# Two more groups of w2's sums made during attention, K's token sums merged into one tile, z on the scalar engine, first results turned at a later step

## The chip, the cores and the metric

One core of one Trainium2 chip runs the whole kernel. The metric is the device time of one launch in microseconds. TensorE (PE in the profile) does the matrix products, VectorE (DVE) and ScalarE (ACT) the elementwise work, GpSimd (POOL) small operations and one of the DMA queues, and SyncE (SP) issues most other DMAs. Each engine works through its own instructions strictly in the order in which the kernel wrote them, so an instruction that waits holds up everything behind it on its engine.

## The reference, cut to what matters

```python
# x: 2048 tokens x 512; H = 32 heads of 16; F = 1792; all float32
h   = layernorm(x) * (1 + ca) + sa            # sa, ca, ga, sb, cb, gb = silu(c) @ w_mod
q, k, v = h @ wqkv                            # per head
pq, pk = phi(q), phi(k)                       # phi(t) = (t + 1 if t > 0 else exp(t)) + 1e-6
kv  = sum over tokens of pk * v               # 16 x 16 per head
z   = sum over tokens of pk                   # 16 per head
o   = (pq @ kv) / (pq . z + 1e-6)
x   = x + ga * (o @ wo)
h   = layernorm(x) * (1 + cb) + sb
x   = x + gb * (mish(h @ w1 + b1) @ w2)
```

## The kernel before, in words

**Precision.** Products run in float32r, which keeps fewer bits than float32. Each operand is therefore split into an upper and a lower part: `split` (L144 to L157) rounds a tile to float32r (the upper part, names ending in `h`, mostly on ACT) and subtracts (the lower part, names ending in `l`, on DVE). A product takes three matmuls: upper by upper, upper by lower, lower by upper.

**Stages.** The 2048 tokens are four blocks `b` of 512, each of four tiles `t` of 128. (1) Normalisation, K and the sums `gacc` over tokens, block by block. (2) z and Q of blocks 0 and 1 (`q_sevens`), the small matrices `kv` and `m`. (3) Attention for each block: `attend` makes the denominators (`den`, then `rden`), sends them through DRAM (`rden_d`) and reads them back spread over partitions (`rd`), scales and splits q (`qs`); `o_unit` multiplies. (4) The MLP. (5) The last down products and the output.

**Seven products for eight.** Q of blocks 0 and 1, and both layers of the MLP, multiply two by two blocks with seven products in place of eight. The sums and differences of blocks that this needs have short names: s1 to s4 for the left operand, t1 to t4 for the right. For the down layer the right operand is w2, in seven groups `g` of two 128-row slices. From its raw rows `w2_blocks` and `blocks_job` make the plain blocks (stored to DRAM as `w2d`), and `sums_job` (L1425) makes the differences: two loads `w2q` for groups from `EARLY` = 3 on (the first three reuse the rows loaded for the plain blocks), four subtractions of 128x256 on DVE (L1446), two roundings on ACT (L1292), two subtractions of 128x512 for the lower parts (L1298, tiles `t_3l` and so on by group number), and four stores to DRAM (`w2t`, L1456). `right_job` (L1461) loads them back as `wt_m` when a product needs them. For groups from `EARLY` on, the right operand of the product `m4` comes straight from SBUF in the first pass.

**z before.** `k_post` makes phi(k) of one tile into `ku[b, t]`. For blocks 1 and 2 an accumulating DMA on the POOL queue adds `ku[b, t]` to `ku[0, t]` (L382); for block 3, DVE does (L380). So four tiles remain. `z_unit` sums each over its 128 tokens with a matmul against 32 columns of ones, the four results lying in four quarters of the partitions; ACT and DVE split the result into `zsum`; `z_side` adds the quarters with two more matmuls (`zbc`, L786), and then DVE makes four diagonals, scales the four parts of `hmask`, and makes the four `zs` tiles.

**Order.** Up to the MLP the order is written out in the code. Steps are Python generators; `spawn` hands one over and `tick` advances all of them by one step after each unit of PE's work. In the MLP a planner (`add_job`, `best_job`, `drive`) writes the order: each job has an earliest time and a due time, worked out from a model with the constants in `T`, and of the jobs that can start on an engine the one with the earliest due time is written next. The model's time is not the chip's; only the order reaches the chip. Two streams feed PE: `main_stream` (up products, PSUM tiles `p_a`, `p_s`) and `fill_stream` (down products, tiles `pa`, `pb`, `pc`, `pd`), for the token blocks 0 and 1 (`L` = 0) and then 2 and 3 (`L` = 2).

**Results.** `result_job` (L1640) gathers a finished down product on DVE (L1645, tile `q`), turns it by a 32x32 transpose (L1656, tile `turned`) and adds it to the tokens in DRAM with accumulating DMAs on POOL (L1666, `x1d<-turned`).

**SBUF.** Nearly all tiles of 128x512 come from one pool of 93 slots (`SLOTS`). A new tile takes a slot that an older one gave up, and its first instruction waits until the last use of the older tile, which can be a DMA that still reads it, has ended.

**Steps that the change and the prediction touch.** The ticks inside `q_sevens`: `result` adds the kept copy on DVE (`cq`, L490) and spawns `phi`, whose exp and relu run on ACT (L370, L371); `copy` (tile `qu`, L497) keeps an unfinished sum on ACT before PE adds the next product to the same PSUM tile. `beside_q` loads the residual rows `r` (L165) on SP, and `mod_side` loads `wm` (L176).

The functions that the diff touches, and what calls them, with the line numbers of the profile:

## Time and profile before

| | us |
|---|---|
| median of 3 runs (lowest, highest) | 481.19 (481.16, 481.33) |
| profiled execution, its own time | 481.08 |
| its span | 479.4 |
| PE busy in the span | 469.5 |
| DVE busy in the span | 421.7 |
| ACT busy in the span | 322.0 |
| POOL busy in the span | 161.0 |

The span runs from the first to the last instruction of the profiled execution; 1.7 us of its own time lies outside. An engine's busy time is the union of its instructions. Matmuls overlap, so a record of one 128x512 float32r matmul shows 0.39 us while one starts every 0.23 us. The granted TensorE clock is 0.998.

### The profile page before, as it was taken

The page shows a single profiled execution, that of the slowest core. Times are in us where ns is not written, and L with a number is a line of the kernel's source. Part 1 is how long each engine was busy: PE and PEld are TensorE (multiplying, and loading weights), DVE is VectorE, ACT ScalarE, POOL GpSimd, SP SyncE. Part 2 cuts the span into 40 slices and gives each one's busy share as a digit, 9 for nine tenths or more (in the row PEclk, how much of TensorE's full clock was granted, in tenths as well). Part 3 has the DMA queues.
Part 4 walks back from the last instruction along what each step waited for, and adds up shares of the span by engine and source line. Part 5 has one row for each costly group of instructions (what it writes and reads, how often), then busy time and mean ns, then how long its engine had stood idle before and what let it go on. Part 6 is the DMA issues. An engine that isn't in the chain of part 4 may idle for free.

```text
span 479.4 us, 7265 instructions
## 1 busy us (share of the span) xinstructions
PE 469.5 (98%) x2300; PEld 385.4 (80%) x2300; DVE 421.7 (88%) x825; ACT 322.0 (67%) x586; POOL 161.0 (34%) x238
## 2 busy tenths in 40 slices
PE   8999999999999999999999999998999999999996
PEld 6788887877887888888888888786888888888886
DVE  6989999899789898999979999998986686989995
ACT  6777686865653988769979999476557566547150
POOL 4583320000022413233542132632331236638430
PEclk9999999999999999999999999999999999999999
DMA  8997689143895446545999373996341469999987
GB/s 310 401 355 210 178 163 270 30 148 94 284 210 150 143 152 226 170 135 179 256 349 308 116 219 121 252 290 217 109 155 51 125 176 244 221 319 242 370 156 162
DMA packets 78881, 99.07 MB, mean 207 GB/s; under 512 B 31538, under 2 KB 51770, under 8 KB 78811
## 3 DMA queue, kind: packets, MB, share of 16 engines
q1 hardware_dynamic: 51528, 54.42, 37.3%
q0 software_dynamic: 24000, 43.15, 34.7%
q10 hardware_dynamic: 3314, 1.05, 1.0%
q8 instruction: 18, 0.29, 0.3%
q14 instruction: 21, 0.16, 0.1%
HBM read 71.31 MB, written 34.61 MB: 221 GB/s over the span
## 4 chain that ended last, share of the span: by engine, by line
PE 80%; DVE 7%; DMA 4%; issue 3%; ACT 2%; SPq 2%; POOL 1%; ACTq 0%; POOLq 0%; DVEq 0%
PE p_a L1515 18%; PE pa L1600 12%; PE p_s L1515 7%; PE pc L1600 6%; PE pb L1600 4%; PE o L142 3%; PE o L140 3%; PE pq_a L479 3%; PE o L141 3%; PE pd L1600 2%; SPq L337 2%; PE pk L140 2%; PE pk L142 2%; PE pk L141 2%; PE gacc L141 1%
## 5 line engine op out<-in xcount | busy, mean ns | idle before, releaser
L1530 ACT ACTIVATE u<-p_a 128x512 f32<-128x512 f32 x42 | 24.9, 594 | 27.1 <-PE p_a L1515 24.6
L1474 POOL DMA_DIRECT2D wt_m<-w2t x36 | 27.9, 1031 | 42.5 <-PE pc L1600 12.6
L1539 ACT ACTIVATE u_a<-c_a,b1c 128x512 f32<-128x512 f32 x42 | 30.1, 719 | 15.5 <-DVE c_a L1536 13.8
L1666 POOL DMA_DIRECT2D x1d<-turned x20 | 23.3, 1732 | 29.0 <-DVE turned L1656 22.2
L1536 DVE TENSOR_TENSOR c_a<-p_s,u 128x512 f32<-128x512 f32 x28 | 19.2, 686 | 14.0 <-PE p_s L1515 9.8
L1489 DVE TENSOR_TENSOR u_a<-u_a,u_a 128x512 f32<-128x512 f32 x28 | 18.2, 681 | 0.0
L1474 POOL DMA_DIRECT2D wt_m<-w2d x16 | 13.3, 1105 | 13.5 <-DVE s_5l L1298 5.5
L277 POOL TENSOR_TENSOR rs_n<-rs_n,half 128x1 f32<-128x1 f32 x16 | 10.7, 668 | 21.1 <-DVE rs_n L303 10.0
L921 POOL DMA_DIRECT2D rden_d<-rden x2 | 1.4, 712 | 47.8 <-DVE rden L919 47.8
L1316 POOL DMA_DIRECT2D w1p<-w1d x16 | 14.0, 981 | 10.3 <-PE p_a L1515 3.7
L946 POOL DMA_DIRECT2D x1d<-r x15 | 8.5, 564 | 22.9 <-DVE r L950 14.9
L370 ACT ACTIVATE e_k<-pk 128x512 f32<-128x512 f32 x15 | 8.9, 593 | 10.7 <-PE pk L142 10.7
L373 DVE SCALAR_TENSOR_TENSOR ku<-e_k,relu_k 128x512 f32<-128x512 f32 x15 | 10.7, 713 | 2.9 <-ACT relu_k L371 2.9
L277 POOL TENSOR_TENSOR rs_x<-rs_x,half 128x1 f32<-128x1 f32 (+1 forms) x10 | 7.7, 780 | 15.9 <-DVE rs_x L272 14.6
L933 DVE SCALAR_TENSOR_TENSOR q<-q,rd 128x512 f32<-128x512 f32 x16 | 10.6, 687 | 2.5 <-DMA rd<-rden_d 2.5
L382 POOL DMA_DIRECT2D ku<-ku x8 | 7.1, 890 | 16.5 <-DVE ku L373 16.5
L373 DVE SCALAR_TENSOR_TENSOR q<-e_q,relu_q 128x512 f32<-128x512 f32 x16 | 10.7, 685 | 2.1 <-ACT relu_q L371 2.1
L1567 ACT ACTIVATE u_a<-p_a,b1c 128x512 f32<-128x512 f32 x14 | 9.6, 682 | 4.4 <-PE p_a L1515 4.3
L1536 DVE TENSOR_TENSOR c_a<-p_a,u 128x512 f32<-128x512 f32 x14 | 9.6, 683 | 3.1 <-PE p_a L1515 2.6
L1634 ACT ACTIVATE U<-pa,mc 128x512 f32<-128x512 f32 x10 | 6.8, 684 | 7.9 <-PE pa L1600 7.9
L1292 ACT ACTIVATE l_m_6h<-u_a 128x512 fp32r<-128x512 f32 x12 | 7.3, 620 | 5.1 <-PE pc L1600 5.1
L253 DVE SCALAR_TENSOR_TENSOR wm<-wm,sc_row 128x512 f32<-128x512 f32 x16 | 10.5, 676 | 0.0
(1465 smaller groups left out, 1883.3 us busy)
## 6 DMA issues: line engine op xcount, KB each, us to landing
wt_m<-w2t POOLq DMA_DIRECT2D x36, 256.0 KB, 5.7
r<-in_x_dram SPq DMA_DIRECT2D x16, 256.0 KB, 3.8
w1p<-w1d POOLq DMA_DIRECT2D x16, 256.0 KB, 5.0
wt_m<-w2t SPq DMA_DIRECT2D x16, 256.0 KB, 9.9
wt_m<-w2d POOLq DMA_DIRECT2D x16, 256.0 KB, 6.6
x<-in_x_dram SPq DMA_DIRECT2D x15, 256.0 KB, 5.4
x1d<-r POOLq DMA_DIRECT2D x15, 256.0 KB, 3.2
w1d<-in_w_dram SPq DMA_DIRECT2D x4, 896.0 KB, 6.6
```

Of the source, the lines that this page charges most:

```text
L140: pe.matmul(o, st[0], mv[0], start=start, stop=False)
L141: pe.matmul(o, st[0], mv[1], start=False, stop=False)
L142: pe.matmul(o, st[1], mv[0], start=False, stop=stop)
L277: pool.tensor_tensor(y, y, half[:, lo:hi], op=ALU.pow)
L373: dve.scalar_tensor_tensor(dst, e, 1.0, r, op0=ALU.min, op1=ALU.add)
L1474: q.dma_start(f32(v), (w2d if src == "w2d" else w2t)[g][:, :, part, :])
L1515: pe.matmul(p, st, mv, start=onto is None and c == 0 and i == 0, stop=c == 1 and i == 2, skip_group_check=onto is not None)
L1530: act.activation(t["u", n], t["pa"], AF.Copy)
L1536: dve.tensor_tensor(t[key], t[p], t["u", n], op=ALU.add)
L1539: act.activation(u, t[key], AF.Mish, bias=b1c[:, f:f + 1])
L1600: pe.matmul(o, st[:, cs], mv, start=not onto and n == 0 and k == 0, stop=n == G - 1 and k == 2, skip_group_check=onto)
L1666: q.dma_start(rows_, sq, accum_op=ALU.add)
```

## The change

Three things are done, and the planner's constants are set anew.

1. **Sums of w2 for groups 3 and 4** (`FIRST`) are made by a new generator, `sums_first`, during attention: two SP loads, four DVE subtractions, two roundings on ACT, two lower parts on DVE and four stores on POOL for each group. The planner starts its own `sums_job` at group 5. For groups 3 and 4 `m4`'s right operand is now loaded from `w2t`.
2. **K's token sums** go into one tile `ku[0, 0]`: more accumulating DMAs (eleven, eight before) merge the tiles, DVE merges block 3's. `z_unit`, one step later, takes one matmul against 128 columns of ones; the two `zbc` matmuls and the split go. In `z_side` the four `zs` and the four `hmask` scalings move from DVE to ACT. In `q_sevens`, `phi` of block 0's summed results waits one tick more.
3. **Results of the down products** are turned in a job of their own, due 6.0 (L = 0) or 2.0 (L = 2) model microseconds after the gather, and the gathered tile reuses the kept one's slot. Before, the turn followed the gather under the gather's due time.

```diff
  'lead_a': 4,
- 'lead_l': 16,
+ 'lead_l': 15,
  'lead_r': 11,
...
  'out_due': 59.4,
- 'out_at': 19.3,
+ 'out_at': 20.3,
  'early_due': 96.7,
  'early_at': -1.3,
- 'norm_due': 60.3,
+ 'norm_due': 60.2,
  'norm_at': 18.7,
...
  'squares_due': 89.9,
- 'turn_due': 82.3,
+ 'turn_due': 83.0,
  'turn_step': 1.0,
...
  'left_early': 17.4,
- 'right_due': 1.2,
+ 'right_due': -0.3,
  'right_early': 13.6,
...
  'sum_early': 14.4,
- 'pace_a': 5.6,
+ 'pace_a': 5.2,
  'pace_l': 3.2,
...
  'copy_due': 12.9,
- 'result_due': 3.7,
+ 'result_due': -0.7,
  'soon': 9.5,
...
  'half_due': 6.5,
- 'sums_late': 4.0,
+ 'sums_late': 3.4,
+ 'first': 2,
+ 'turn_late': [6.0, 2.0],
  'left_out': 10.0,
- 'add': 0.1}
+ 'add': 2.8}
 
...
     make_identity(nc, ident)
-    w32 = cst.tile([P, P], F32R, name="w32")
     bmask = cst.tile([P, P], F32, name="bmask")
...
     def make_constants():
-        pool.memset(f32(w32), 1.0 / 32)
+        pool.memset(ztiny, S * TINY)
         pool.memset(kv, 0.0)
...
 
-    def phi(p, name, dst, wait=False):
-
-        if wait:
+    def phi(p, name, dst, wait=0):
+
+        for _ in range(wait):
             yield
...
         if b == NB - 1:
-            dve.tensor_tensor(ku[0, t], ku[0, t], ku.pop((b, t)), op=ALU.add)
+            if 0 < t < 3:
+                dve.tensor_tensor(u, u, ku.pop((b, t - 1)), op=ALU.add)
+            if t == 3:
+                for i in 2, 3:
+                    dve.tensor_tensor(ku[0, 0], ku[0, 0], ku.pop((b, i)), op=ALU.add)
+        elif b == 1:
+            pool.dma_start(ku[0, t], ku.pop((b, t)), accum_op=ALU.add)
         elif b:
-            pool.dma_start(ku[0, t], ku.pop((b, t)), accum_op=ALU.add)
+            if t < 2:
+                pool.dma_start(ku[0, t], ku.pop((0, t + 2)), accum_op=ALU.add)
+            pool.dma_start(ku[0, (1, 0, 0, 1)[t]], ku.pop((b, t)), accum_op=ALU.add)
 
...
 
-    zsum = [sb(f"zsum_{i}", F32R) for i in range(2)]
+    ztiny = cst.tile([P, 1], F32, name="ztiny")
+    zbc = sb("zbc_sb")
 
...
 
+        u = ku.pop((0, 0))
         p = ps("h", "z")
-        for t in range(4):
-            pe.matmul(p[32 * t:32 * (t + 1), :], ones[:, 0:32], ku.pop((0, t)), start=True, stop=True)
-        act.activation(zsum[0], p, AF.Copy)
-        dve.scalar_tensor_tensor(zsum[1], p, S * TINY / 4, f32(zsum[0]), op0=ALU.add, op1=ALU.subtract)
+        pe.matmul(p, ones, u, start=True, stop=True)
+        act.activation(zbc, p, AF.Identity, bias=ztiny[:, 0:1])
 
...
             pq[b, g] = sb(f"q_{b}_{g}")
-            spawn(phi(p, f"q_{b}_{g}", pq[b, g], u is not None))
+            spawn(phi(p, f"q_{b}_{g}", pq[b, g], 0 if u is None else 1 + (b == 0)))
 
...
 
-        zbc_ps = ps("tp", "zbc")
-        for i in range(2):
-            pe.matmul(zbc_ps, w32, zsum[i], start=i == 0, stop=i == 1)
-        zbc = sb("zbc_sb")
-        act.activation(zbc, zbc_ps, AF.Copy)
-        yield
+        for k in range(4):
+            zs[k] = sb(f"zs_{k}")
+            act.activation(zs[k], zbc, AF.Copy, scale=mc[:, k:k + 1])
+            if k == 1:
+                yield
         for g in range(4):
...
                                      accum_out=zc[:, g:g + 1])
-            dve.tensor_scalar(hmask[:, g, :], hmask[:, g, :], zc[:, g:g + 1], 1.0, op0=ALU.mult, op1=ALU.mult)
-        for k in range(4):
-            zs[k] = sb(f"zs_{k}")
-            dve.tensor_scalar(zs[k], zbc, mc[:, k:k + 1], 1.0, op0=ALU.mult, op1=ALU.mult)
-
+        for g in range(4):
+            act.activation(hmask[:, g, :], hmask[:, g, :], AF.Copy, scale=zc[:, g:g + 1])
         dve.tensor_reduce(zh, zbc.rearrange("p (h r) -> p h r", r=16), op=ALU.add, axis=mybir.AxisListType.X)
...
                         w1.rearrange("(c k r) f -> c r k f", c=4, r=32)[c])
+
+    def sums_first(g):
+
+        r = [sb(f"w2p_{g}_{i}") for i in range(2)]
+        for i in range(2):
+            f = 2 * g + i
+            sp.dma_start(r[i], w2[P * f:P * (f + 1), :])
+        yield
+        t12, t34 = [sb(f"t{m}_{g}") for m in (12, 34)]
+        b11, b12, b21, b22 = [nat(v, h) for v in r for h in (0, 1)]
+        t1, t2, t3, t4 = [lin(v) for v in (t12[:, 0:H], t12[:, H:D], t34[:, 0:H], t34[:, H:D])]
+        for d, u, v in (t1, b12, b11), (t2, b22, t1), (t3, b22, b12), (t4, b21, t2):
+            dve.tensor_tensor(d, u, v, op=ALU.subtract)
+        yield
+        keep = {}
+        parts = [split(f"t{i}_{g}", t, keep, i) for i, t in enumerate((t12, t34))]
+        next(parts[0])
+        next(parts[1])
+        yield
+        d = drp.tile([P, 2, 4, H], F32, name=f"w2t_{g}")
+        for i in range(2):
+            run(parts[i])
+            for n in range(2):
+                pool.dma_start(d[:, n, 2 * i:2 * i + 2, :], f32(keep[i][n]).rearrange("p (t c) -> p t c", t=2))
+            if i == 0:
+                yield
+        w2t[g] = d
+
+    FIRST = range(EARLY, EARLY + T['first'])
 
...
                 load_wqkv(0, t)
+            if last and t == 0:
+                pool.dma_start(ku[0, 0], ku.pop((0, 1)), accum_op=ALU.add)
             if last and t < 2:
...
                     spawn(split(f"wq_{k}", wraw[0, k], wq, k))
-                if t == 2:
+                if t == 3:
                     z_unit()
-                if t == 3:
                     spawn(z_side())
...
             load_x(2, n - 4, "r")
+        if n == 3 and T['first']:
+            next(firsts[0])
         if n == 1:
...
 
+    firsts = [sums_first(g) for g in FIRST]
     q_sevens(beside_q)
+    if T['first']:
+        next(firsts[0])
     load_x(2, 3, "r")
...
     next(attending)
+    if T['first']:
+        next(firsts[0])
+        spawn(firsts[0])
     for g in range(4):
...
         q_unit(3, g)
+        if T['first'] > 1:
+            if g == 0:
+                next(firsts[1])
+            if g == 2:
+                spawn(firsts[1])
         tick()
...
                  "hf": lambda: k[1] < 2 and tuple(k[1:]) in hf, "r": lambda: k[2] in ("m1", "m2") and tuple(k[1:]) in right, "w2d": lambda: k[1] == 0 and 0 in w2d,
-                 "w2r": lambda: k[1] == 0 and 0 in w2d}
+                 "w2r": lambda: k[1] == 0 and 0 in w2d, "w2t": lambda: k[1] in FIRST}
         if k[0] in there and there[k[0]]():
...
         def gather(i):
-            q[i] = sb(f"q_{L}_{n}_{c}_{i}")
-            dve.scalar_tensor_tensor(q[i], bank[L, place][i], gate(c, i), us[L, i], op0=ALU.mult, op1=ALU.add)
+            q[i] = us.pop((L, i))
+            dve.scalar_tensor_tensor(q[i], bank[L, place][i], gate(c, i), q[i], op0=ALU.mult, op1=ALU.add)
 
...
 
-        for i in range(2):
-            yield d_(lambda i=i: turn_(i), makes=[("t", L, n, c)] if i else ())
-        if n and c:
-            return
-        lo, hi = (0, P) if n else (64 * c, 64 * (c + 1))
-        for k in range(4):
-            def put(q, k=k):
-                sq, rows_ = strip_squares(turned[L, n], x1d[L + n], k, lo, hi)
-                q.dma_start(rows_, sq, accum_op=ALU.add)
-            yield dma_(put, [("sum", L, n, c)] if k == 3 else (), [("t", L, n, 1)] if n else (), queue=POOL, size=ADD)
+        def turns():
+            for i in range(2):
+                yield d_(lambda i=i: turn_(i), makes=[("t", L, n, c)] if i else ())
+            if not (n and c):
+                yield from puts()
+        def puts():
+            lo, hi = (0, P) if n else (64 * c, 64 * (c + 1))
+            for k in range(4):
+                def put(q, k=k):
+                    sq, rows_ = strip_squares(turned[L, n], x1d[L + n], k, lo, hi)
+                    q.dma_start(rows_, sq, accum_op=ALU.add)
+                yield dma_(put, [("sum", L, n, c)] if k == 3 else (), [("t", L, n, 1)] if n else (), queue=POOL, size=ADD)
+
+        add_job(turns(), now[0] + T['turn_late'][1 if L else 0])
 
...
 
-        ahead, loaded, summed = 0, 0, EARLY
+        ahead, loaded, summed = 0, 0, EARLY + len(FIRST)
         rows01 = []
...
                     if units[loaded][0] or units[loaded][1] not in ("m1", "m2", "m4") or (
-                            units[loaded][1] == "m4" and units[loaded][2] < EARLY):
+                            units[loaded][1] == "m4" and units[loaded][2] < EARLY + len(FIRST)):
                         need = now[0] + at_[loaded] - at_[k] - T['right_due']
```

## The prediction

> **What bounds the kernel.** I read the page first, then the waits of PE, then busy time by stretches of 20 us, then the order of DVE, ACT and SP around each wait.
>
> ```profile
> PE 469.5 (98%) x2300; PEld 385.4 (80%) x2300; DVE 421.7 (88%) x825; ACT 322.0 (67%) x586; POOL 161.0 (34%) x238
> ...
> PE pc L1600 <- DVE l_m_0l L1298: 1.8, 1, 1.8
> PE p_a L1515 <- DVE t_1l L1298: 1.1, 1, 1.1
> ...
> PE pq_a L479 <- ACT qu L497: 0.7, 1, 0.7
> PE o L142 <- DVE qs_2l L154: 0.4, 1, 0.4
> ...
> 100.00:120.00 20.00, 19.27 (x88) 14.77 (x87) 19.31 (x47) 11.32 (x22) 0.00 (x0) 1.00 0.41 117
> ...
> 140.00:160.00 20.00, 19.64 (x113) 15.49 (x114) 19.13 (x37) 9.71 (x20) 5.53 (x10) 1.00 0.62 145
> 160.00:180.00 20.00, 20.00 (x120) 16.38 (x119) 16.55 (x38) 17.46 (x37) 5.20 (x10) 1.00 0.47 152
> ...
> 300.00:320.00 20.00, 18.85 (x83) 15.05 (x83) 19.35 (x41) 11.64 (x20) 10.95 (x16) 1.00 1.05 272
> 320.00:340.00 20.00, 18.24 (x81) 14.75 (x80) 17.19 (x32) 12.87 (x24) 5.82 (x9) 1.00 0.67 212
> ...
> 460.00:480.00 20.00, 15.23 (x107) 14.16 (x105) 12.84 (x23) 1.45 (x3) 3.04 (x4) 0.94 0.68 130
> ```
>
> PE is the bound. It lacks 479.4 - 469.5 = 9.9 us of the span. The end takes 19.4 - 15.23 = 4.2 of it and the start most of the rest of what can't be had; the four waits in the fence, 0.73, 0.36, 1.15 and 1.76 us by their stretches (20 less PE's column, the first after the length), make 4.0. A change gains by work taken from PE or by those four waits; anything else that it saves is beside PE. The two late waits end on DVE, which is busy 19.35 of 20 us there.
>
> **z on PE.** Before, the four-quarter product takes 1.00 us of PE and `zbc` 0.46. Now there is one plain float32 product of 128x512, 128 columns wide.
>
> ```profile
> 100.27 1.00 PE z L429 x8
> ...
> 104.22 0.46 PE zbc L786 x2
> ...
> 6.42 1.17 PE L211 MATMUL warm<-ones 128*128 128x128 f32 x8
> ...
> 4.59 2.04 PE L220 MATMUL sc_bc<-c,halves 128*128 128x512 f32 x2
> ```
>
> The nearest row is the warm-up: four plain float32 products of 128 columns each, as much in sum as one of 512, in 1.17 us. The same shape once, in the launch's first microseconds, took 2.04. So the new z costs 1.0 to 2.04; I take 1.10. PE gains 0.46 - 0.10 = **0.36 us** (bounds +0.46 and -0.58). Its sums are ready: one DVE addition more (0.6) stands before it, and it starts twelve `gacc` products (12 x 0.23 = 2.7 us) later than before. The accumulating DMAs form a chain, each waiting for the one before on its tile:
>
> ```profile
> 87.22 0.56 POOL L537 DMA_DIRECT2D ga_d<-ga_row  x1 [11.49 <-ACT ga_row L535]
> ...
> ku<-ku POOLq DMA_DIRECT2D x8, 256.0 KB, 4.0
> ```
>
> POOL's last addition of before is issued 11.49 us ahead of `ga_d`, at 75.7. The chain after it is two landings longer, some 5 us each with the issue, and ends near 86; POOL has the 11.49 us free, and z is needed after 100. Cost nothing; if the chain were 14 us longer, z would be late one for one. The Trainium skill ("DMA: Bandwidth & Descriptors", Rules for kernel authors) asks for that chain: an accumulating DMA must wait for the earlier one's semaphore. No run here shows what happens without.
>
> **z beside PE, and the wait in `q_sevens`.** PE's 0.73 us ends on `qu`. On ACT that copy stands behind an exp that waits for DVE's `cq`, and `cq` (113.93) stood behind `z_side`.
>
> ```profile
> 114.65 0.63 ACT L370 ACTIVATE e_q<-cq 128x512 f32<-128x512 f32 x1 [1.13 <-DVE cq L490]
> 115.71 1.06 ACT L497 ACTIVATE qu<-pq_a 128x512 f32<-128x512 f32 x2
> ...
> 110.30 1.67 DVE L797 TENSOR_SCALAR zs<-zbc_sb,mc 128x512 f32<-128x512 f32 x4
> ...
> 113.93 0.68 DVE L490 TENSOR_TENSOR cq<-pq_a,qu 128x512 f32<-128x512 f32 x1
> ...
> L1634 ACT ACTIVATE U<-pa,mc 128x512 f32<-128x512 f32 x10 | 6.8, 684 | 7.9 <-PE pa L1600 7.9
> ```
>
> The extra tick puts the two `qu` ahead of exp and relu, 1.06 us by the starts of the rows, more than the wait. DVE also loses 1.67 for `zs` and the scalings of `hmask`. Gain **0.73**. ACT takes on four `zs`, 4 x 0.684 by the nearest scaled copy, 2.7 us, and four scalings of 128x32, less than that each, 1.0 us at a guess; its column leaves 20 - 11.32 = 8.7 us idle here. If they stood before a `qu` and the copies came no earlier, the wait would stay and could double: bounds +0.73 and -0.73 (rival 3 holds the wait kept). The Trainium skill ("ScalarE: Activation LUTs", Rules for kernel authors) speaks against this move: add and mul belong on VectorE. The trace agrees on the price of one, 0.68 against DVE's 1.67 / 4 = 0.42; by the rule the move is a loss of some 1.1 us on ACT, but it counts only if ACT ends a wait of PE. The later exp and relu of block 0 come one tick nearer to `den`, which needs their q, but not after those of its last results. Cost nothing; without that cover `den` and PE wait for a tick's work, a microsecond.
>
> **Sums of groups 3 and 4: what it removes.** In the planner's part: 8 subtractions at 0.41, 4 lower parts at 0.68, by the starts of back-to-back rows (0.33 and 0.60) 8 x 0.33 + 4 x 0.60 = 5.0 us of DVE; 4 roundings of ACT; 4 loads and 8 stores of 256 KB. Added there: 2 loads of `wt_m`.
>
> ```profile
> 298.12 0.69 DVE L1656 STREAM_TRANSPOSE turned<-q 128x512 f32<-128x512 f32 x1
> ...
> 300.84 0.68 DVE L1298 TENSOR_TENSOR t_1l<-t_t,t_1h 128x512 fp32r<-128x512 f32 x1
> ...
> 309.67 0.42 DVE L1446 TENSOR_TENSOR t<-w2q 128x256 f32<-128x256 f32 x1
> 310.00 0.68 DVE L1298 TENSOR_TENSOR t_3l<-t,t_3h 128x512 fp32r<-128x512 f32 x1
> 310.61 0.41 DVE L1446 TENSOR_TENSOR t<-w2q,t 128x256 f32<-128x256 f32 x1
> ...
> 321.19 0.69 DVE L1298 TENSOR_TENSOR s_1l<-s,s_1h 128x512 fp32r<-128x512 f32 x1 [1.14 <-DMA w2t<-t_5h]
> ...
> 326.48 0.43 DVE L1298 TENSOR_TENSOR a_1l<-w1p,a_1h 128x256 fp32r<-128x256 f32 x1 [1.25 <-DMA w2t<-t_6h]
> 326.82 0.69 DVE L1298 TENSOR_TENSOR l_m_0l<-s,l_m_0h 128x512 fp32r<-128x512 f32 x1
> ```
>
> The largest wait of PE (1.76) is `l_m_0l`. DVE ran late to it for two reasons: the sums just before, and two halts (1.14 and 1.25) in which a new tile waited for the slot of an older one that a `w2t` store still read. With 5.0 us of sums gone and half the stores, DVE is some 6 us earlier; **1.76** goes in full. Next would be the other operands of the same products, so +1.76 and 0 are the bounds.
>
> **The later turn.** The 1.15 us end on `t_1l`, which DVE ran 2.7 us after two transposes; six later, they fall behind it: 2 x 0.6 = 1.2 us. But PE arrives here 0.36 + 0.73 earlier than before, and the DVE work ahead, which PE's products release, follows only in part. I take **half, 0.6** (bounds +1.15 and 0). In the last stage the transposes come about 2 us later.
>
> ```profile
> 464.84 3.04 POOL L1931 DMA_DIRECT2D rows<-x1d  x4 [8.31 <-DMA x1d<-turned]
> ...
> 471.01 0.43 DVE L1962 TENSOR_TENSOR rows<-rows,q_last 128x256 f32<-128x256 f32 x1
> ...
> rows<-x1d POOLq DMA_DIRECT2D x4, 128.0 KB, 3.4
> ```
>
> The first of the four `rows` loads landed near 468.3 and is used at 471.0; so 2 us fit into 2.7, and on POOL nothing stands behind them. Cost nothing; beyond 2.7 us the additions of the rows would move, and the end only when the last one does.
>
> **What attention takes on.** For group 3: 2 loads on SP after the residual row of step 3; 4 subtractions (1.3 us) on DVE ahead of `kv`; 2 roundings on ACT; 2 lower parts (1.2 us) and 4 stores (2.2 us of POOL, 0.55 each an estimate by the issue of `ga_d`, 0.56) in the next two ticks. Group 4 the same, a block later.
>
> ```profile
> 114.04 1.24 SPq L165 DMA_DIRECT2D r<-in_x_dram  x2
> 118.47 0.80 SPq L176 DMA_DIRECT2D wm<-wmd  x2
> ...
> SPq L165 <- PE pq_a L479: 7.9, 3, 6.2
> ...
> w2q<-in_w_dram SPq DMA_DIRECT2D x4, 256.0 KB, 5.2
> ...
> 127.86 0.86 DVE L1058 TENSOR_TENSOR kv<-kv_ps,bmask 64x256 f32<-64x256 f32 x2 [2.34 <-PE kv_ps L1055]
> ...
> 135.19 6.28 DMA rd<-rden_d
> 141.50 0.69 DVE q L933
> ```
>
> DVE idled 2.34 us before `kv`: the subtractions fit, if the rows are there by 126.5. Issued near 115 and landing in 5.2 us they are. The lower parts meet the halts before the first two `q`, of which the second (141.5) waits for `rd` and not for DVE, so they shift nothing behind it. The `wm` loads behind them on SP (118.5) come later by two slots' waits, under DVE work that can follow `kv`. POOL is busy 5.53 of 20 us in 140:160, so four stores fit, behind the issues of `rd`. But they share the DMA engines with the `rd` loads, on which the chain to `qs_2l`, PE's 0.36, hangs: I take **-0.2** (bounds +0.36, and -1.8 by the largest single wait of before). Group 4 falls into 160:180, where DVE has 20 - 16.55 = 3.4 us free for its 2.5; cost nothing, and without that cover they stand ahead of block 2's `qs`.
>
> **The constants.** PE waits nowhere between 160 and 300 (the four waits lie outside), so a new order can gain nothing there and can lose. The adds `c_a` are due 4.4 us later, loads up to 1.5, accumulating DMAs are held for longer. Bounds 0 and -1.8 again; I take 0, since the planner starts no product before its PSUM tile is free.
>
> **Sum.** 0.36 + 0.73 + 1.76 + 0.6 - 0.2 = 3.25 us. The profiled execution took 481.08 (span 479.4 and 1.7 around it), 0.11 below the median: 481.08 - 3.25 = 477.83, with that 0.11 **477.9 us**.
>
> **Rivals.**
> (1) The waits move on. DVE was busy 97% and 86% of these two stretches, so the next late operand may stop PE as long as the last did, and time won at 115 is waited for at 300. Then of the sum only z stays: 481.2 - 0.36 = 480.8, and with half of the late waits back (2.9 / 2) 479.4. For it: two unlike operands ended the two waits. Against: 7 us of DVE's load and halts leave that stretch.
> (2) Slower: SP's slots. SP waited 6.2 us in one piece for a slot in this stretch; if the group's loads wait so, they are issued near 121 and land near 126.5, and by each microsecond past 126.5 `kv`, `rden`, `rd` and `qs_2l` are late, and PE with them. It decides when it eats the 3.25: landing near 129.8. With the 6.2 twice (issue 127.4, landing 132.6) the chain is 6.1 late: 477.9 + 6.1 = 484.0.
> (3) The new z is as slow as the launch's one (2.04) and the kept `qu` wait stays: 477.9 + 0.9 + 0.7 = 479.5.
>
> **Chances.** Forecast, 476.4 to 479.2: 0.53. Part of it back (rivals 1 and 3), 479.2 to 480.2: 0.16. Rival 1 in full, within 0.2% of 481.19 (480.2 to 482.2; about what a measurement here can tell from no change): 0.15. Slower, rival 2 or a wait that the new order makes: 0.16. So faster 0.69, same 0.15, slower 0.16. All four waits and z's best give 481.2 - 4.0 - 0.46 = 476.7; a little below stands for the profile's rounding. The range 476.3 to 482.2 leaves out 0.16 above and 0.03 below; the forecast's own is 476.4 to 479.2.
>
> **What would show it.** z: one product of 1.0 to 1.2 us, no `zbc` product. `q_sevens`: no wait of PE for `qu`. 300 to 340: PE's two columns from 37.1 to near 39.5 us, no DVE halt on a `w2t` store, DVE idle there. Attention: the subtractions before `kv`, and `kv` within 0.5 us of the end of its product; a `kv` or `rd` later than that, or PE waits for `c_a`'s tiles between 160 and 300, make the prediction wrong.

## The result, and the profile after

The changed kernel takes 484.96 us (median of 4 runs, 483.87 to 485.27), the kernel before beside it 481.18 (480.85 to 481.33): 1.0076 times as long, 95% interval 1.0058 to 1.0093. The forecast was 477.9 with a range of 476.3 to 482.2. The change made the kernel slower, by about as much as it was to make it faster. The profiled execution of after took 485.19 us, its span is 483.5.

The busy times of the page and the waits of PE (total in us, number, longest), after:

```profile
PE 471.2 (97%) x2292; PEld 385.6 (80%) x2292; DVE 420.1 (87%) x816; ACT 324.1 (67%) x593; POOL 160.2 (33%) x236
```

```profile
PE pa L1648 <- DMA wt_m<-w2t: 2.4, 1, 2.4
...
PE o L144 <- DVE qs_2l L156: 1.0, 1, 1.0
...
PE o L142 <- ACT qs_2h L150: 0.7, 1, 0.7
PE gacc L143 <- DVE pk_3l L158: 0.7, 1, 0.7
```

Of the four waits that the forecast counted, three are gone: `qu`, `t_1l` and `l_m_0l` are in the list no more. The fourth, `qs_2l`, has grown from 0.36 to 1.0 and has `qs_2h` beside it. At the top stands a wait that the kernel before did not have: the last stage's product `pa` for a load of `wt_m`. PE's busy time grew by 1.7 us although it has eight instructions fewer; part of PE's work ran slower.

Five places in PE's work, each marked by the start of one product, say where the time went. The rows are of after's timeline (start, duration):

```profile
127.16 0.50 PE L142 MATMUL pq<-hT_x_0h,wq_0h 128*128 128x512 f32 x1
...
200.89 0.39 PE L1563 MATMUL p_a<-b_0h,a_0h 128*128 128x512 f32 x1
...
425.48 0.39 PE L1648 MATMUL pb<-l_m_5h,wt_m 128*128 128x512 f32 x1
...
454.56 0.39 PE L1648 MATMUL pd<-l_m_5h,wt_m 128*128 128x512 f32 x1
...
469.05 0.28 PE L142 MATMUL m<-wt_m,l_m_6h 128*128 128x256 f32 x1
```

The same products in before, and in two of the experiments told below:

| product | before | after | after - before | e13 | e15 |
|---|---|---|---|---|---|
| first of Q, block 2 | 127.74 | 127.16 | -0.58 | 126.69 | 127.29 |
| first up product | 198.67 | 200.89 | +2.22 | 197.61 | 198.24 |
| last of `pb` | 426.69 | 425.48 | -1.21 | 422.68 | 423.84 |
| last of `pd` | 455.25 | 454.56 | -0.69 | 451.24 | 452.40 |
| first `m` of the last stage | 465.00 | 469.05 | +4.05 | 460.99 | 462.15 |

Read by differences: up to 127 PE has won 0.6; attention loses 2.8; the stretch with the two late waits wins 3.4; from there to the last of `pd` 0.5 is lost, and in the last stage 4.7. The span is 4.1 longer.

**The last stage.** Three views of after: one line of the chain of waits; POOL's and PE's timeline (start, duration; in brackets the idle time before and what ended it); and a window of 2 us with its granted clock (the seventh figure):

```profile
450.48 10.64 DMA wt_m<-w2t
```

```profile
446.57 1.06 POOL L1978 DMA_DIRECT2D out_dram<-x1d  x1 [5.69 <-DMA x1d<-turned]
448.09 0.52 POOL L1781 DMA_DIRECT2D out_dram<-x1d  x1 [0.45 <-DMA wt_m<-w2t]
450.48 0.75 POOL L1522 DMA_DIRECT2D wt_m<-w2t  x1 [1.87 <-ACT l_m_0h L1340]
...
461.16 0.50 PE L1648 MATMUL pa<-l_m_4h,wt_m 128*128 128x512 f32 x1 [2.42 <-DMA wt_m<-w2t]
...
462.21 0.63 PE L1648 MATMUL pa<-l_m_5l,wt_m 128*128 128x512 f32 x1
462.64 0.63 PE L1648 MATMUL pa<-l_m_5h,wt_m 128*128 128x512 f32 x1
...
465.62 0.40 PE L1648 MATMUL pa<-l_m_1h,wt_m 128*128 128x512 f32 x1
```

```profile
462.00:464.00 2.00, 2.00 (x7) 1.58 (x6) 0.69 (x1) 0.00 (x0) 0.00 (x0) 0.54 1.31 248
```

On POOL's queue a copy of finished token rows to the output (L1978) stood 5.69 us for the accumulating DMAs that it must not overtake. The last load of `wt_m` from `w2t` was queued behind both copies, then waited another 1.87 us for its slot, and was issued at 450.48. In before, POOL issued its last such load at 442.49, and the copies went out on SP:

```profile
442.49 0.70 POOL L1474 DMA_DIRECT2D wt_m<-w2t  x1 [0.57 <-PE pa L1600]
...
442.26 5.91 SPq L1729 DMA_DIRECT2D out_dram<-x1d  x2
```

In the changed kernel the load landed after 10.64 us, beside the two copies' own traffic (POOL's seven loads of this kind in 436 to 460 of before: median 6.5), and PE stopped for 2.42 us. How much of the lateness is queue, slot and landing these rows don't divide; e1 below takes the first away. After the stop, from 462.21 on, a product starts every 0.43 us instead of every 0.23, for 3.41 us: eight products, 8 x 0.20 = 1.6 us more. The window shows the granted clock at 0.54. Stop and slow stretch make 4.0 of the 4.7.

**Attention.** POOL's, ACT's and DVE's timeline of after, and the window 140:160 (PE's busy time is its second figure):

```profile
134.02 2.40 POOL L960 DMA_DIRECT2D rd<-rden_d  x4 [3.49 <-DMA rden_d<-rden]
136.39 0.61 POOL L841 DMA_DIRECT2D w2t<-t_3h  x1
...
138.07 0.56 POOL L841 DMA_DIRECT2D w2t<-t_3l  x1
...
152.65 2.39 POOL L960 DMA_DIRECT2D rd<-rden_d  x4 [6.28 <-DMA rden_d<-rden]
...
142.80 0.63 ACT L150 ACTIVATE qs_0h<-q 128x512 fp32r<-128x512 f32 x1 [3.81 <-DMA w2t<-t_3l]
...
127.28 0.86 DVE L1098 TENSOR_TENSOR kv<-kv_ps,bmask 64x256 f32<-64x256 f32 x2 [0.60 <-PE kv_ps L1095]
...
143.41 0.69 DVE L374 SCALAR_TENSOR_TENSOR q<-e_q,relu_q 128x512 f32<-128x512 f32 x1 [2.25 <-DMA w2t<-t_3h]
```

```profile
140.00:160.00 20.00, 18.32 (x106) 13.77 (x105) 17.07 (x33) 7.69 (x16) 3.65 (x6) 1.00 0.67 206
```

Group 3's four stores could be issued only when POOL's queue was through its wait for `rden_d`, at 136.39 to 138.07. They took 5.7 to 5.9 us to land. Until then the tiles `t_3h` and `t_3l` held their slots, and two new tiles that were to get these slots made ACT stand 3.81 us, to 142.80, and DVE 2.25, to 143.41. What followed on DVE, the second block's `rden` among it, came later, and POOL's second `rd` was issued at 152.65 instead of 148.33. PE waited for `qs_2h` and `qs_2l` in 140:160. The row of before:

```profile
148.33 2.35 POOL L925 DMA_DIRECT2D rd<-rden_d  x4 [3.30 <-DMA rden_d<-rden]
```

**Where the forecast held.** z, and the two late stretches, which were 18.85 and 18.24 us busy before:

```profile
104.09 1.02 PE L439 MATMUL z<-ku,ones 128*128 128x512 f32 x2
```

```profile
100.00:120.00 20.00, 20.00 (x88) 16.13 (x87) 18.57 (x41) 15.01 (x31) 0.00 (x0) 1.00 0.45 135
...
300.00:320.00 20.00, 20.00 (x89) 16.31 (x88) 17.11 (x34) 11.58 (x21) 9.89 (x13) 1.00 0.93 210
320.00:340.00 20.00, 20.00 (x90) 16.42 (x89) 18.55 (x35) 12.81 (x23) 4.91 (x7) 1.00 0.59 185
```

### The profile page after: what moved, and what is told of

Read it like the earlier page. It is cut to its first block, busy times and chain, and to the rows that moved or that the text cites. A ratio compares the mean times of both kernels' runs of the same rounds, so it can differ in the third digit from the quotient of the medians.

```text
span 483.5 us, 7247 instructions
## 1 busy us (share of the span) xinstructions
PE 471.2 (97%) x2292; PEld 385.6 (80%) x2292; DVE 420.1 (87%) x816; ACT 324.1 (67%) x593; POOL 160.2 (33%) x236
## 3 DMA queue, kind: packets, MB, share of 16 engines
q10 hardware_dynamic: 3314, 1.05, 1.0%
## 4 chain that ended last, share of the span: by engine, by line
PE 72%; DVE 10%; DMA 5%; issue 4%; ACT 4%; SPq 2%; POOL 1%; ACTq 0%; POOLq 0%; DVEq 0%
PE p_a L1563 20%; PE pa L1648 10%; PE p_s L1563 8%; PE pc L1648 6%; PE pb L1648 4%; PE pq_a L488 3%; DMA wt_m<-w2t 2%; PE pd L1648 2%; SPq L338 2%; PE pk L143 2%; PE pk L144 2%; PE pk L142 2%; PE gacc L143 1%; PE gacc L144 1%; PE gacc L142 1%
## 5 line engine op out<-in xcount | busy, mean ns | idle before, releaser
L1522 POOL DMA_DIRECT2D wt_m<-w2t x26 | 23.2, 1146 | 44.8 <-PE pc L1648 9.2
L1364 POOL DMA_DIRECT2D w1p<-w1d x17 | 12.9, 762 | 17.8 <-DVE t_6l L1346 4.5
L1522 POOL DMA_DIRECT2D wt_m<-w2d x14 | 11.8, 1058 | 12.2 <-PE p_a L1563 6.2
L981 POOL DMA_DIRECT2D x1d<-r x15 | 8.4, 561 | 18.8 <-DVE r L985 10.1
L1340 ACT ACTIVATE l_m_0h<-u_a 128x512 fp32r<-128x512 f32 x12 | 7.5, 626 | 4.4 <-DVE u_a L1537 4.4
L1541 DVE TENSOR_TENSOR s<-u_a,u_a 128x512 f32<-128x512 f32 x14 | 8.8, 685 | 0.9 <-DMA w2t<-t_6l 0.9
```

Of the source, the lines that this page charges most:

```text
L1522: q.dma_start(f32(v), (w2d if src == "w2d" else w2t)[g][:, :, part, :])
```

## The experiments

Two theories stood after this reading. A: the constant `add` = 2.8 (the planner's price of an accumulating DMA) brings the copies onto POOL and with them the late load. B: group 3's stores, put on POOL's queue behind a wait, hold slots for too long. The rivals: the cost lies in the other constants, in DVE's added work in attention, in the later turns, or in the copies' queue alone. All ratios are to the kernel before, timed beside it on the same chip, with their 95% intervals. "Old constants" means the nine numbers of `T` that the diff changes, put back (`add` 0.1 among them); `first` and `turn_late` are named apart.

### The last stage: the copies, the constant and the wait

**e1.** The copies go to SP's queue, the constants stay.

```diff
-size=8 * LATE)]), now[0] + T['out01'])
+size=8 * LATE, queue=SP)]), now[0] + T['out01'])
...
-(), [("sum", L, 0, 0)])]), now[0] + T['left_out'])
+(), [("sum", L, 0, 0)], queue=SP)]), now[0] + T['left_out'])
```

> The changed kernel with one edit: the three late copies of x1d to out_dram are pinned to SP's queue (two of them stood on POOL's, one of these 5.69 us waiting for accumulations with the wt_m load of group 4's m7 behind it). Theory (late load): that load is issued by 447 and no longer at 450.48, PE's wait of 2.42 us at 461.2 is gone and with it the 4.4 us at half pitch behind it, about 2.0 us more: 484.96 - 4.4 = 480.5 us, between 479.6 and 481.5. Rival (crowding): the copies and accumulations fill the 16 DMA engines whichever queue issues them, and the load still lands after 459: 483.5 to 485. Rival (the later turn itself): the load is on time, but the accumulations' end sets the rows, and the end stays within 1 us: 484 to 485.

486.69 us, 1.0107 [1.0084, 1.0131]. The wait for `w2t` is gone, and one on SP's own loads has come. PE's waits and SP's timeline:

```profile
PE m L142 <- DMA wt_m<-w2d: 3.0, 2, 2.8
```

```profile
446.02 7.77 SPq L1781 DMA_DIRECT2D out_dram<-x1d  x1
...
453.91 4.33 SPq L1522 DMA_DIRECT2D wt_m<-w2d  x6
```

SP was held 7.77 us by the issue of one copy, and its six loads started at 453.91 (448.26 in before). On POOL the last load from `w2t` now went out at 448.47, 2.0 us earlier, and was in time. With the copies off its queue that load is no longer late, but another queue alone is no cure: at this place in the order a copy delays whatever stands behind it. I had expected the queue to be the whole of it, and that was wrong.

**e2.** The changed kernel with one constant back.

```diff
- 'add': 2.8}
+ 'add': 0.1}
```

> The changed kernel with one constant put back: the planner's cost of an accumulation to x1d, 'add', 0.1 in place of 2.8. Theory (this constant alone puts the copies on POOL): POOL's queue then has no copy to out_dram among the late loads, no wait for wt_m over 0.5 us in the last 50 us, 480 to 481.5 us. Rival (the later turn, right_due or lead_l place them): the copies' wait stays ahead of the load, 484 to 485.3. Rival (the smaller cost lets the accumulations stand before loads elsewhere): the last stage is mended, but a wait for wt_m comes back between 290 and 350, 481.5 to 483.

481.89 us, 1.0005 [0.9983, 1.0028]: 0.7% better than the changed kernel. The copies are on SP again, the 2.4 us wait is gone (0.6 for `w2d` is left in the last stage), and attention's loss stays. The one number carries the loss of the last stage. SP's timeline and PE's waits:

```profile
446.87 5.75 SPq L1781 DMA_DIRECT2D out_dram<-x1d  x2
```

```profile
PE m L142 <- DMA wt_m<-w2d: 0.6, 1, 0.6
```

**e3** and **e5.** The kernel before with all nine new constants, and with `add` = 2.8 alone.

> The kernel before with only the nine constants of the change (add 2.8, right_due -0.3, result_due -0.7, lead_l 15 and the rest), none of its new code. Theory (constants make the loss): a copy to out_dram stands on POOL ahead of wt_m loads of the last stage there too, and PE waits 1 to 3 us for one, with or without the half pitch: 482 to 486 us. Rival (the constants need the new code to hurt): 480.5 to 481.8. Rival (constants also remove the late waits that the before has at l_m_0l and t_1l, 2.4 us together): 478.5 to 480.

> The kernel before with one constant changed: 'add' 2.8 in place of 0.1, nothing else. Theory (this one constant makes the last stage's loss): the copy of x1d's left half stands on POOL among the late wt_m loads, a wait of 3 to 6 us for wt_m in the last 50 us with half pitch behind it, as with all nine constants: 486 to 493 us. Rival (it takes right_due or result_due with it): 480.5 to 483.

e3 takes 492.28 us, 1.0221 [1.0202, 1.0240]; e5 488.65 in one run, beside 481.49. PE's waits and POOL's timeline of e3, then PE's waits of e5:

```profile
PE pa L1600 <- DMA wt_m<-w2t: 5.3, 1, 5.3
```

```profile
456.79 1.06 POOL L1926 DMA_DIRECT2D out_dram<-x1d  x1 [2.47 <-DMA rq<-x1d]
```

```profile
PE pa L1600 <- DMA wt_m<-w2t: 2.2, 1, 2.2
```

The same wait in the old code, with none of the new sums, z or turns: it comes from the constant. In e3 the copy at 456.79 stands ahead of the load at 458.06. e3 lies above the range that I had given it, and some 3.6 us above e5, so in the old code the other eight constants seem to cost something too; with e5 run once, that is not shown.

**e7.** The changed kernel, but PE is given nine products with a zero weight tile where it waits.

```diff
+                if (L, name, g, i) == (2, "m7", 4, 0):
+                    for _ in range(9):
+                        pe.matmul(o, none, left[L, name, 3][0], start=False, stop=False, skip_group_check=True)
```

> The changed kernel with nine more products, weights all zero, added to pa ahead of the first product of m7's group 4 in the last stage: they fill 2.0 of the 2.42 us in which PE waits for the load. Theory (the half pitch of 4.4 us behind the wait comes from the idle stretch itself): the products behind stay at a pitch of 0.23 us, and the wait costs 2.4 us and no more: 484.96 - 2.0 = 483.0, between 482.3 and 483.8. Rival (the half pitch comes at that place whether PE has been idle or not): 484.5 to 485.6.

483.99 us in one run (span 482.3, after's 483.5). PE's timeline:

```profile
459.05 2.20 PE L1651 MATMUL pa<-l_m_3h,none 128*128 128x512 f32 x9
461.58 0.50 PE L1653 MATMUL pa<-l_m_4h,wt_m 128*128 128x512 f32 x1 [0.32 <-DMA wt_m<-w2t]
...
462.61 0.39 PE L1653 MATMUL pa<-l_m_5l,wt_m 128*128 128x512 f32 x1
```

The load lands as late as in after, but every product behind it keeps its 0.23 us. From the last of `pd` (455.03 here) to the first `m` (467.85) it takes 12.82 us; after takes 14.49, 1.67 more. The slow stretch is a consequence of PE's idling, not of the late data, and costs some 1.6 us of its own, as the count of products said. The span shows less of it, because this execution has a slow stretch in attention that after's has not, behind the two waits for `qs_2`. Its window, with the clock at 0.50:

```profile
152.00:154.00 2.00, 2.00 (x7) 1.54 (x6) 2.00 (x7) 0.00 (x0) 2.00 (x5) 0.50 0.50 97
```

### Attention: where, when, and which part of the new sums

**e6.** Old constants; group 3's sums move to the Q products of block 3, group 4's to the `o` products of block 1.

```diff
-        if n == 3 and T['first']:
-            next(firsts[0])
...
+            if n == 4:
+                next(firsts[1])
             if n == 5:
                 spawn(attend(3, 3, sp))
+            if n == 6:
+                spawn(firsts[1])
```

> The changed kernel's code with the constants of before, and with groups 3 and 4 later: group 3 is loaded, subtracted and stored beside block 3's q (where group 4 stood), group 4 beside block 1's o products. To be held against the same code with only 'add' put back (481.9 us, PE waits of 1.0 and 0.7 us for qs_2l and qs_2h). Theory (group 3's stores hold slots that DVE, ACT and SP wait for between 139 and 143 us, so the reciprocal and rd come late): these two waits are gone and no w2t store stands in front of a reciprocal: 479.4 to 480.5. Rival (DVE has no room anywhere there, so the wait moves to qs of another block, to n or to tp_n): 481 to 482.5. Rival (group 4 so late brings the late waits at l_m_0l and t_1l back): 481.5 to 483.

481.92 us, 1.0003 [0.9985, 1.0021]. PE's idle time in 120 to 165 falls from after's 1.7 to 0.7 us, but 1.7 us of it appears in 165 to 200 (0.4 in after): the loss moved with the groups. PE's start-up part was also 1.5 us slower in this profile. This placement is no cure.

**e8** and **e10.** Old constants, no sums in attention (`first` 0); e10 turns at once as well (`turn_late` [0, 0]).

> The changed kernel's code with the constants of before and no early groups: sums of groups 3 to 6 all in the MLP as before, so what is left of the change is z and the later turn. Theory (groups 3 and 4 remove the two late waits and cost 1.9 us in attention): the waits for l_m_0l and t_1l are back, 2 to 3 us together, the waits for qs_2 are gone: 480.3 to 481.3, as with z alone (480.9). Rival (the later turn removes the late waits by itself): 478.3 to 479.5.

> As the run without groups (483.6), constants of before, but with no delay of the turns (0 and 0): only the delay differs between the two. Theory (the delay moves turns among the sums of groups 3 to 6, DVE waits there for w2t stores, and two waits of PE close together bring half pitch): 480.3 to 481.5, as z alone. Rival (not the delay but the result written over its own input, or a run's chance): 482.8 to 484.2.

e8: 483.62 us, 1.0038 [1.0012, 1.0064]; e10: 481.56 us, 0.9984 [0.9970, 0.9998]. Without the groups attention has no loss, and the late waits are back: 1.4 for `l_m_0l` in both, 1.2 for `t_1l` in e10. So the sums' removal from the planner's part is what ends `l_m_0l`. And the later turn by itself is a loss of 0.54% between the two (I had expected e8 at 480.3 to 481.3): in e8's profile two waits follow each other closely, and the clock falls. That this makes the whole 0.54% is not shown. PE's timeline and a window of e8:

```profile
322.87 0.50 PE L1563 MATMUL p_s<-t_0h,s_1l 128*128 128x512 f32 x1 [0.87 <-DVE s_1l L1346]
...
325.72 0.62 PE L1648 MATMUL pc<-l_m_0l,wt_m 128*128 128x512 f32 x1 [1.42 <-DVE l_m_0l L1346]
```

```profile
326.00:328.00 2.00, 2.00 (x6) 1.51 (x6) 1.41 (x3) 0.00 (x0) 0.00 (x0) 0.50 1.04 394
```

**e9.** Both groups as in the change, old constants, `turn_late` [0, 0].

> The changed kernel's code with the constants of before and no delay of the turns (turn_late 0 and 0), so that z and the two early groups are what is left of the change. To be held against the same with only 'add' put back and the later turns (481.9). Theory (the later turn costs: without groups it made 483.6 against 480.9 for z alone, and the groups gain 1.7 on top): 479.2 to 480.6, below both kernels. Rival (with the groups' sums out of DVE's way the later turn is free): 481.5 to 482.5. Rival (the later turn is what removes t_1l's wait, as the prediction has it by half): a wait of about 1.1 us for t_1l near 300, 482 to 483.

482.35 us, 0.9998 [0.9979, 1.0018]. The wait for `t_1l` is back with its whole 1.2 us, `l_m_0l` is not: the two waits have different causes, and the later turn removes the first in full. In time e9 is no slower than e2 (1.0005), which has the later turns and the other eight new constants. What the later turn is worth with both groups, no pair of runs that differ in it alone shows. PE's wait:

```profile
PE p_a L1563 <- DVE t_1l L1346: 1.2, 1, 1.2
```

**e11** and **e14.** One group only (3, at block 3's Q), old constants; e11 turns at once, e14 turns later ([6, 2]).

> As the run with turns at once, but only group 3 is done early, beside block 3's q where group 4 stood; group 4 is done in the MLP as before. Theory (each early group costs its 3.0 us on a DVE that is over 90% busy in attention, and each takes one late wait away): between the run without groups and the run with two, 480 to 481, with one late wait of 0.5 to 1.5 us left. Rival (the slot stall of the early place was the main cost, and one group is enough for the late waits): 478.5 to 479.8.

> One early group (group 3, beside block 3's q, where it made PE idle only 0.14 us between 165 and 200), constants of before, and the later turns of the change, which with two groups keep t_1l's wait of 1.2 us away. If the late waits depend on the place of the turns, they are gone or under 1 us here: 479.8 to 481. If it takes both groups out of the MLP (rival), 2 to 3 us of waits stay between 290 and 340, with half pitch where two come close together: 482 to 484.

e11: 482.53 us, 1.0009 [0.9989, 1.0028], above both ranges that I had given, with waits of 1.9 for `c_a` and 1.2 for `t_1l`. e14: 479.09 us, 0.9945 [0.9925, 0.9965]; of the late waits 0.08 us is left. With one group moved, the later turn is worth 0.64%; with none (e8, e10) it costs 0.54%. The two parts need each other, and one group is enough for it.

**e12.** What in group 3's work costs: e10, with group 3's loads, subtractions and splits made and thrown away, and no stores.

```diff
-            for n in range(2):
-                pool.dma_start(d[:, n, 2 * i:2 * i + 2, :], ...)
...
-        w2t[g] = d
```

> As the run without groups and turns at once (481.6; PE idle 0.5 us between 120 and 165), plus group 3's loads, four subtractions and two splits at the changed kernel's place beside block 2's q, their results thrown away: the same DVE and ACT work and no stores to w2t, which is done in the MLP as there. Theory (the stores hold slots, DVE, ACT and SP halt for them between 139 and 143): without stores no halt, PE idle 0.4 to 0.8 us between 120 and 165, 481.3 to 482. Rival (the 3.0 us of DVE work is what delays the reciprocal): PE idle 1.4 to 1.9 us there, as in the changed kernel (1.68), 482.6 to 483.2.

481.75 us, 1.0001 [0.9981, 1.0020]. In attention PE idles 0.2 us in 120 to 165 (0.5 in e10, 1.7 in after). All of group 3's work on DVE and ACT is there, and attention loses nothing (the 0.17% between the two medians is within the intervals): the rival "DVE's added work" falls; the stores are left.

**e13.** Old constants, both groups, later turns; group 3's four stores on SP.

```diff
-                pool.dma_start(d[:, n, 2 * i:2 * i + 2, :], ...)
+                (sp if g == EARLY else pool).dma_start(d[:, n, 2 * i:2 * i + 2, :], ...)
```

> The changed kernel's code with the constants of before (later turns kept), and group 3's four stores issued by SP instead of POOL, where they stood behind the waits for the reciprocal and rd until 136.4. If slots are the cause and SP is free, they land before 138, DVE does not halt at 141 and qs_2's two waits (1.0 and 0.7) go: 479.5 to 481. Rival (SP stands halted itself between 130 and 142, so they go no earlier): as with the stores on POOL, 481.5 to 482.3, or slower where SP's next loads wait behind them.

477.88 us, 0.9931 [0.9911, 0.9952]. SP's and DVE's timeline, then two windows:

```profile
126.29 0.32 SPq L841 DMA_DIRECT2D w2t<-t_3h  x1
...
135.67 0.32 SPq L841 DMA_DIRECT2D w2t<-t_3l  x1
...
140.61 0.69 DVE L374 SCALAR_TENSOR_TENSOR q<-e_q,relu_q 128x512 f32<-128x512 f32 x1
...
141.59 0.95 DVE L954 RECIPROCAL rden<-rden 128x128 f32<-128x128 f32 x1
```

```profile
120.00:140.00 20.00, 20.00 (x198) 16.27 (x197) 18.58 (x42) 12.24 (x23) 3.14 (x5) 1.00 0.81 255
140.00:160.00 20.00, 20.00 (x116) 15.90 (x115) 19.93 (x40) 11.21 (x24) 5.86 (x10) 1.00 0.73 227
```

The first store leaves 10.1 us earlier than in after, `q` (143.41 in after) starts at 140.61 with no halt before it, the second reciprocal at 141.59, and PE is busy 20.00 of 20 us in both windows (18.32 in the second in after). That is theory B.

### The parts alone and together

**e4.** The kernel before with the merged K sums, the new z and the later `phi`, and nothing else.

> The kernel before with only the sums of K merged into one tile, the single z product without the second product and the extra tick ahead of q's first phi; constants, groups 3 and 4 and the turns as before. The prediction has z at +0.36 us of gain and the qu wait at 0.73: 481.18 - 1.1 = 480.1. If the 1.3 us that the changed kernel loses before 90 us comes from the merged sums on DVE and POOL, little is left: 480.6 to 481.3. If it comes from elsewhere (other parts, or differences between runs), the whole of what the two traces show between 90 and 119 us is gained, 1.9 us: 479.0 to 479.8.

480.91 us, 0.9985 [0.9969, 1.0001]. The `qu` wait is gone; a new one of 1.5 us for `pk_3l` stands ahead of the last `gacc` products in this profile. Of the 1.1 us that this part was to bring, 0.7 is seen (0.15% of 481.6), and the interval just includes none.

**e15** and **e16.** The changed kernel with both edits (`add` 0.1, group 3's stores on SP), and with the stores alone.

> The changed kernel with two edits and nothing else: 'add' 0.1, and group 3's four stores issued by SP. If these two are the whole of its loss, it comes to what the run with all of the constants of before had (477.9): 477.3 to 479.5, PE idle under 0.5 us between 120 and 165 and no wait for wt_m over 1 us at the end. If the other eight constants matter (rival), 480 to 482.

> The changed kernel with one edit: group 3's stores issued by SP; 'add' stays 2.8. Theory (two separate losses that add up): attention is mended (PE idle 1.7 to 0 between 120 and 165), the late load, its wait of about 2.4 us and the half pitch stay: 485.0 - 1.7 = 483.3, between 482.3 and 484.3. Rival (the last stage's late load follows the transfers' times, and what is gained in attention is lost or gained there): under 481.5 or over 484.8.

e15: 478.83 us beside 482.07, 0.9939 [0.9917, 0.9962]; e16: 481.72, 0.9997 [0.9976, 1.0018]. PE's timeline of e16:

```profile
457.92 0.79 PE L1648 MATMUL pa<-l_m_4h,wt_m 128*128 128x512 f32 x1 [2.45 <-DMA wt_m<-w2t]
458.52 0.63 PE L1648 MATMUL pa<-l_m_4l,wt_m 128*128 128x512 f32 x1
```

e16 mends attention (its first up product starts at 197.56, after's at 200.89) and keeps the last stage's stop and slow stretch, here at once. Its time is below the range that I had given to two separate losses (482.3 to 484.3), which took attention's loss as PE's 1.7 us of idle time and not as the 2.8 us between the markers. The four cases stand like a small table:

| | `add` 2.8 | `add` 0.1 |
|---|---|---|
| stores on POOL | 1.0076 (the change) | 1.0005 (e2) |
| stores on SP | 0.9997 (e16) | 0.9939 (e15) |

Each edit is worth 0.6 to 0.8%, with or without the other; the two causes are separate and add up. Two stretches between the markers above say the same without the medians. From the first Q product of block 2 to the first up product, before takes 70.9 us and after 73.7; e2, with the stores on POOL, takes 74.5, and with the stores on SP e13 and e15 take 70.9 and e16 71.0. From the last of `pd` to the first `m`, before takes 9.75 us and after 14.49; e16, with `add` 2.8, takes 14.79, and with `add` 0.1 e2, e13 and e15 take 9.75 each.

e13, which has all the old constants, is as fast as e15 within the intervals, so in the new code the other eight constants are worth nothing that these runs can tell. e13, e14 and e15 beat both kernels. In e15's last stage PE no longer waits (18.41 busy in after); its window:

```profile
440.00:460.00 20.00, 20.00 (x90) 16.57 (x89) 19.29 (x33) 7.08 (x12) 9.46 (x12) 1.00 1.10 313
```

## Why the prediction was wrong

By its own steps:

- **z on PE, +0.36:** right. One product in two records, 1.02 us in all where 1.10 was taken; `zbc` is gone.
- **The `qu` wait, +0.73:** right; 100:120 is 20.00 busy (19.27 before), and ACT took the scaled copies without PE waiting for it. By the marker at 127 the two brought 0.58 of 1.09. The rest is in PE's start-up part, whose idle time differs between profiles of the same code (1.7 us before 90 in before's profile, 2.8 in e3's), and in a new wait for `pk_3l` (0.7), for which the prediction had no step. That wait is 0.3 to 2.1 us in eleven of the fifteen profiles with the merged sums, and at most 0.2 in the three with the old ones.
- **`l_m_0l`, +1.76, and the later turn, +0.6:** the mechanism was right, the second was mis-sized. Both waits are gone, 2.9 us where 2.36 was taken, and the later turn removes the 1.15 whole (e9 has it back). That DVE would not halt on `w2t` stores there was wrong, but the halts that are left reach no product.
- **Attention, -0.2:** the step that failed first. It cost 2.8 us, beyond even its bound of -1.8. The prediction looked for the cost in the loads, which were in time (`kv` came at 127.28, 0.58 earlier than before), and in shared DMA engines. It put the four stores "behind the issues of `rd`" and called that a fit because POOL had idle time in 140:160. But the stores came to POOL before 140, where its idle time was the wait for `rden_d` (3.49 us, the row at 134.02), and its queue is in order: stores behind it are late, their tiles keep their slots, and the next owners of the slots are attention's own `qs` and `q`. Idle time in an engine's column is not room on its queue. The Trainium skill ("DMA: Bandwidth & Descriptors", Anatomy of one DMA) says that a semaphore wait happens on the issuing sequencer before dispatch; the rows at 134.02 and 136.39 agree: the first store went out 2.37 us after the first `rd`, right behind the fourth.
- **The constants, 0:** the step that failed most. `add` alone costs 0.7% (1.0076 against 1.0005), some 3.4 us, in the last stage. (The markers give 4.7, but e2's profile takes 2.2 us longer than after's behind the first `m`.) The prediction looked for new waits only in 160 to 300 and gave as a bound the largest wait of before, 1.8. The place to look was where accumulations and loads share POOL's queue at the end, and the price was not the wait alone: the slow stretch after it added some 1.6 (e7, and the count of products).
- **"On POOL nothing stands behind them"**, and two more loads of `wt_m` at nothing: wrong in the same place. A load did stand behind a copy that waited for the accumulations, and landed slowly beside it.
- **Group 4 in 160:180, 0:** nearly right: PE idles 0.4 us in 165 to 200, and e13 and e15 have 0.14 and 0.19.

Rival 2 gave 484.0, close to the time that came, by another mechanism: slots were late indeed, but those held by the stores and not those that the loads waited for, and they cost 2.8 us where it had 6.1; the last stage, which it did not name, cost more. With both failed steps mended the forecast's total comes out: e15's median is 3.2 us below the kernel before's, and 3.25 was the sum. By its terms that is partly luck. In e15's profile z and the `qu` wait bring 0.45 where 1.09 was taken, and the stretch with the two late waits 2.4 where 2.36 was; its span is 2.3 us shorter.

## What to carry to other kernels

Before a DMA is costed at nothing, read what its queue is waiting for at that place and which tile stays occupied until it lands: an engine that idles in a wait has no room for what is queued behind that wait. A number in a planner's model is a change of the order everywhere that number is used, so its cost is looked for in each stage where such instructions share a queue, and above all in the last, where nothing comes after to make up for it. Parts that pay only together (the sums moved and the turns delayed) should be tried together and apart, and one bad constant can hide a good change.

## What was not expected of the hardware

**A stop of PE can cost more than its length.** After a stop of 2.42 us the products ran at half pitch for 3.41 us, with the clock at 0.54; after 2.45 us in e16 and 2.21 in e5 likewise. In e8 two waits of 0.87 and 1.42 us, both within 4 us, were enough (0.50 in 326:328), and in e7 and e9 the two waits for `qs_2`, 0.7 and 0.95 us, did it in attention (0.50 in 152:154). The same two waits in after, e1 and e2 did not, nor did a single stop of 1.76 us (before, `l_m_0l`). So the same stop can cost its length or some 1.6 us more. The Trainium skill ("TensorE: Matmul & The Clock Gate", Part 1: The HAM clock gate) gives some 3.4 us both for the idle window after which the clock falls and for the busy one after which it is whole again. The second agrees with the 3.41 us here, but the slow stretches of e1 (after a stop of 2.77 us) and e3 (after 5.27) lasted 5.7 and 6.0. The first does not agree, since less idle time than that was enough in seven of these kernels. In after the stretch began 1.05 us after the end of the wait, in e16 at once; what decides whether and when it begins, no run here shows.

**The issue of a copy from DRAM to DRAM can hold SP for long.** One full-row copy to the output took SP 7.77 us in e1, and two of them 5.91 in before, but POOL 0.52 (448.09). SP is not always held: of the two in before one took 0.54 us and the other 5.27, and in e1 the first such copy, at 436.47, took 0.59. What makes the difference was not tried.
